# One 128-row transfer for each of the last output tiles instead of two of 64 rows, with a new order list for the compute jobs, in an attention and SwiGLU kernel

## The chip, the core and the metric

The kernel runs on one core of a Trainium2 chip. A core has a matrix engine (TensorE, in the profile PE, its weight loads PEld), a vector engine (VectorE, DVE), a scalar engine (ScalarE, ACT), a general engine (GpSimd, POOL) and a queue engine (SyncE, SP). Each runs its own list of instructions in order and waits for others through semaphores. Transfers to and from memory are issued here from the lists of SP, ACT and POOL, and all are carried by the same 16 DMA engines. Matrix products land in PSUM, which has eight banks of 128 rows by 512 floats; everything else on the chip lives in SBUF, 128 rows (partitions) wide.

The metric is device time in microseconds (us) of one execution, as the median of several runs. Lower is better.

## The reference

A linear attention with cosine weights feeds a SwiGLU block. Batch is 8, heads 8, sequence 576, head size 64; the block has 4608 tokens, width 512 and inner width 1536.

```
phi(x)  = concat(relu(x) * cos_w, relu(x) * sin_w)        # cos_w, sin_w by position
kv      = einsum('bhsf,bhsd->bhfd', phi(k), v)
z       = sum over s of phi(k)
num     = einsum('bhsf,bhfd->bhsd', phi(q), kv)
den     = einsum('bhsf,bhf->bhs',  phi(q), z) + 1e-6
x       = (num / den), heads side by side                 # [4608, 512]
g       = x @ w_gate
out     = (silu(g) * (x @ w_val)) @ w_out                 # [4608, 512], float32
```

## The kernel before

**Tiles and groups.** The 4608 tokens are cut into 72 pieces of 64 rows (`NH = B * NC`, `NC = 9` pieces for each batch). A tile `t` (0 to 35) is two pieces, 128 rows: piece `2t` on partitions 0 to 63, piece `2t + 1` on 64 to 127. Four tiles are a group `tg` (0 to 8). The output is seen as `out_v[b, c]`, one 64-row piece of 512 columns each, whose rows lie nine output rows apart.

**Stages.** For each tile the attention numerators and denominators are one PE job (`tile_jobs`, lines 784 and 789 in the profile), ACT and DVE divide (lines 803 to 820), and the result `x` is turned, either by a DMA transpose from SP (`turn_job`, line 749, `xT<-x`) or, for early tiles, by PE (line 757) with a copy by ACT (line 630). For each batch from the second on, `q` is made into features in `r_q`, with nine pieces by ACT (line 890), and turned by one DMA transpose from SP (line 852, `phit<-r_q`). For each group the gate and value products follow (lines 917, 990, 1065), then the output products (line 1275 for group 0, line 1155 for the others).

From group 1 on, products are made with seven block products in place of eight, of sums and differences of blocks. Within gate and value these are M1 to M7 (line 990), whose token-side sums X1 to X4 are made by DVE (`x_sum_jobs`, line 963, tile `kvt`, in the last group `raw_kv`). Within the output these are P1 to P7 (line 1155). M7 needs X3, and X3 needs the turned x of all four tiles of its group. An output block is ready as follows: columns 0 to 255 (`HD = 256`) of a group's first two tiles after P2 (job `e11`), columns 256 to 511 of its last two after P5 (`e22`), columns 0 to 255 of its last two after P4 (`e21`), and columns 256 to 511 of its first two after P3 (`e12`).

**The order of the work.** Work up to about 27 us is issued by a written sequence and stands ahead of the list that follows. All later work is cut into 1453 jobs with numbers in the order of their making. A job has an engine, a function that issues its instructions, and the jobs that it comes after. The string `ORDER` lists all job numbers; a letter picks an engine where there is a choice, and digits behind the colon pick a PSUM bank or another buffer. The jobs are issued in this order, so the list fixes the order on every engine and queue; the waits follow from the data. The numbers in `Job({...})`, `tail=` and `dma=` fed the planner that once wrote the list; as the list is written out, they change nothing in what is issued.

Jobs that the prediction speaks of, by number: 47 is an early output product of group 0 (tile 2, four of the inner chunks; line 1275). 99 turns tile 7's x on PE (line 757) and 100 copies it on ACT (line 630). 124 is the DMA transpose of batch 2's features (SP, line 852), 142 the attention product of tile 9 that reads it (line 789). 348 and 349 are X3 and X1 of group 2 (DVE, line 963), 354 is M7 of group 2 (line 990). 286 is P4 of group 1 (line 1155).

**The stores.** Group 0 stores by `store_jobs` from SP, groups 1 to 6 and the last two tiles of group 7 from POOL, the first two tiles of group 7 (28 and 29) from SP: two transfers a tile, one for each 64-row piece (line 1124). Group 8, the last, stores by blocks as they become ready, half of each from SP (partitions 0 to 63) and half from ACT (64 to 127): `store_two_jobs` (line 1253) moves 64 partitions of two tiles by 256 columns, 128 KB, and `store_tile_jobs` (line 1262) 64 partitions of one tile by 256 columns, 64 KB. So the end of SP's queue holds four issues of group 7 (line 1124) and six of group 8 (two of line 1253, four of line 1262), and the end of ACT's the other six of group 8. In the last group the blocks of `e22`, `e21` and `e12` are evicted by DVE, one tile at a time (lines 1212 and 636), `e11` by ACT (line 632).

Of the kernel before, what the change touches and what calls it, by code (L numbers as in the profile page):

```python
# [18 lines left out]
def kernel(  # L19
# [1098 lines left out]
    def store_jobs(t, after, put, queues, cols=slice(0, d_model)):  # L1118
        for e in range(2):
            q_ = queues[e]  # L1120

            def fn(j, e=e):
                idx = 2 * t + e
                {"POOL": nc.gpsimd, "SP": nc.sync, "ACT": nc.scalar}[j.eng].dma_start(  # L1124
                    out=out_v[idx // NC, idx % NC][:, cols], in_=ob_of(t)[e * SH:(e + 1) * SH, cols])
            Job({q_: 535 if q_ == "POOL" else 610}, fn, after=after, put=put, tail=1500.0, dma=(1450.0, 480.0))
# [6 lines left out]
    def pair_of(p):  # L1133
        return (ob_last if obs[p].kind == "last ob" else ob_all)[:, obs[p].at[0]]

    def out_jobs(tg, key):
# [68 lines left out]
        if last:  # L1205
            store_two_jobs(t0, slice(0, HD), [e11], ("SP", "ACT"))
# [7 lines left out]
        if last:  # L1214
            store_two_jobs(t0 + 2, slice(HD, d_model), e22, ("SP", "ACT"))
# [6 lines left out]
        if last:  # L1222
            for n in range(2):
                store_tile_jobs(t0 + 2, n, slice(0, HD), [e21[n]])
        else:
            for t in (t0 + 2, t0 + 3):
                store_jobs(t, e22 + e21, [rooms[1]], ("POOL", "POOL"))
# [8 lines left out]
        if last:  # L1236
            for n in range(2):
                store_tile_jobs(t0, n, slice(HD, d_model), [e12[n]])
        else:
            for t in (t0, t0 + 1):  # L1240
                store_jobs(t, [e11] + e12, [rooms[0]], ("SP", "SP") if tg == NTG - 2 else ("POOL", "POOL"))
# [5 lines left out]

    def store_two_jobs(t, cols, after, queues):
        for e in range(2):
            def fn(j, e=e):  # L1250
                (b, c), (b1, _) = divmod(2 * t + e, NC), divmod(2 * t + 2 + e, NC)
                assert b == b1
                {"SP": nc.sync, "ACT": nc.scalar}[j.eng].dma_start(
                    out=out_v[b, c:c + 3:2, :, cols].rearrange("c p f -> p c f"),
                    in_=pair_of(t // 2)[e * SH:(e + 1) * SH, :, cols])
            Job({queues[e]: 660}, fn, after=after, tail=1300.0, dma=(700.0, 560.0))

    def store_tile_jobs(t, i, cols, after, queues=("SP", "ACT")):
        for e in range(2):
            def fn(j, e=e):  # L1260
                b, c = divmod(2 * (t + i) + e, NC)
                {"SP": nc.sync, "ACT": nc.scalar}[j.eng].dma_start(
                    out=out_v[b, c][:, cols], in_=pair_of(t // 2)[e * SH:(e + 1) * SH, i, cols])
            Job({queues[e]: 620}, fn, after=after, tail=1300.0, dma=(700.0, 280.0))
# [36 lines left out]
    for lo, hi in ((0, 2), (2, 4)):  # L1301
        def fn(j, lo=lo, hi=hi):
            o = raws[1, "k"][:, lo:hi]
            relu_on(j.eng, o, o)
# [118 lines left out]
    for tg in range(1, NTG):  # L1423
# [43 lines left out]
        6:7 4:6 12:1 8:0 10:5 16:3 20:4 29 5:8 9:7 13:0 17:1 1:3 376 7 187 28 191 11 186 188 189 31 30 24:7 18:2 26:3  # L1467
        22:6 21:6 25:2 33 32 2:7 67:0 34:45 14:1 70a 36a 35a 38a 37a 3 27 380 19 68v 69 15 23 71 0 41:2 44 40:0 43
        72:340 84:7 78:561 39:1 42 73 74 75:3 85a 79 86 80 87v 81:2 88 76:3 77 45 101:7 89:560 95:341 47 90 96 377
        102a 378 91 92:3 97 48 82:5 93:6 55:1 83 94 98:0 192 193 109 190 103 110 113 381 114 46 99:1 51:3 52 49  # L1470
# [105 lines left out]
```

## Time and profile before

| | |
|---|---|
| time, median of 3 runs | 299.13 us (298.21 to 299.59) |
| the profiled execution's own time | 298.66 us |
| its span, first to last instruction | 296.8 us |
| granted TensorE clock, mean | 0.996 |
| transferred | 40.90 MB, 138 GB/s on average |
| stores from POOL (line 1124) | 52 of 128 KB, 532 ns of POOL each |
| stores from SP (line 1124) | 12 of 128 KB |
| DMA transposes of x from SP | 28, 4.1 us from issue to landing in the median |
| DMA transposes of the features from SP | 6, 10.3 us in the median |

How to read the views: in the busy time by stretch a row has its window in us, its length, then for each engine busy time and, in brackets, the count of instructions, then the granted clock, the DMA engines' share and GB/s. In the timeline a row has start, length, engine, line, operation, tiles written and read, and a count where neighbours are merged; in brackets the idle time before it and what ended that. `SPq` and `ACTq` are queue instructions, here issues of transfers. The chain of waits is read as start, length, and what the time went to. A row of DMA issues ends with the median time from issue to landing. In the rows of DMA queues, q1 is SP's queue and q10 ACT's, with packets, MB and the share of 16 engines. A matmul's length in a row holds its way through the array, so neighbours overlap.

### The profile page before, as it was taken

The page shows a single profiled execution, that of the slowest core. Times are in us where ns is not written, and L with a number is a line of the kernel's source. Part 1 is how long each engine was busy: PE and PEld are TensorE (multiplying, and loading weights), DVE is VectorE, ACT ScalarE, POOL GpSimd, SP SyncE. Part 2 cuts the span into 40 slices and gives each one's busy share as a digit, 9 for nine tenths or more (in the row PEclk, how much of TensorE's full clock was granted, in tenths as well). Part 3 has the DMA queues.
Part 4 walks back from the last instruction along what each step waited for, and adds up shares of the span by engine and source line. Part 5 has one row for each costly group of instructions (what it writes and reads, how often), then busy time and mean ns, then how long its engine had stood idle before and what let it go on. Part 6 is the DMA issues. An engine that isn't in the chain of part 4 may idle for free.

```text
span 296.8 us, 8157 instructions
## 1 busy us (share of the span) xinstructions
PE 290.1 (98%) x3292; PEld 237.7 (80%) x3292; DVE 252.9 (85%) x513; ACT 199.1 (67%) x423; POOL 69.1 (23%) x122
## 2 busy tenths in 40 slices
PE   8999999999999999999999999999999999999993
PEld 4697455665877888988898898888988898888882
DVE  7976889889987899999898977998778968968882
ACT  6664347978479868985499689976566555564630
POOL 7963530012015012213343020400050032002000
PEclk9999999999999999999999999999999999999998
DMA  7999999999969999599959947980270036000226
GB/s 255 232 196 198 202 206 209 229 202 155 170 149 171 199 209 144 102 172 148 209 118 159 197 68 131 208 146 2 38 171 8 2 89 127 0 2 18 55 53 161
DMA packets 71973, 40.90 MB, mean 138 GB/s; under 512 B 48768, under 2 KB 68736, under 8 KB 71936
## 3 DMA queue, kind: packets, MB, share of 16 engines
q0 software_dynamic: 24800, 24.39, 49.9%
q1 hardware_dynamic: 46528, 15.47, 27.6%
q10 hardware_dynamic: 608, 0.52, 0.6%
q8 instruction: 26, 0.43, 0.6%
q14 instruction: 11, 0.09, 0.1%
HBM read 37.75 MB, written 9.44 MB: 159 GB/s over the span
## 4 chain that ended last, share of the span: by engine, by line
PE 87%; DMA 9%; DVE 2%; issue 0%; DVEq 0%
PE banks L990 43%; PE banks L1155 23%; DMA xT<-x 4%; DMA phit<-r_q 4%; PE banks L440 4%; PE banks L917 4%; PE banks L1275 3%; PE banks L789 3%; PE banks L718 2%; PE banks L1065 2%; DMA wo_sb<-in_v_dram 1%; DVE v L292 1%; PE banks L371 1%; PE banks L784 1%; PE banks L1323 0%; PE banks L314 0%
## 5 line engine op out<-in xcount | busy, mean ns | idle before, releaser
L1124 POOL DMA_DIRECT2D out_dram<-ob x52 | 27.3, 532 | 128.4 <-ACT ob L632 87.6
L630 ACT COPY banks<-banks 128x512 f32<-128x512 f32 (+1 forms) x53 | 30.4, 577 | 22.3 <-PE banks L990 9.9
L1049 ACT ACTIVATE sg<-banks 128x512 bf16<-128x512 f32 x72 | 40.9, 599 | 5.8 <-PE banks L990 5.6
L1085 DVE TENSOR_TENSOR ht<-sg,banks 128x512 f16<-128x512 bf16 x60 | 40.4, 682 | 4.8 <-PE banks L990 4.4
L1155 PEld LDWEIGHTS <-ht 128*128 128x128 f16 x384 | 37.5, 98 | 4.5
L990 PEld LDWEIGHTS <-wg_sb 128*128 128x128 f16 x384 | 36.7, 98 | 5.3
L990 PEld LDWEIGHTS <-wgs_sb 128*128 128x128 f16 x368 | 35.4, 98 | 6.4 <-issue 0.5
L1010 DVE TENSOR_TENSOR banks<-m,banks 128x512 f32<-128x512 f32 x44 | 30.2, 692 | 7.3 <-PE banks L990 6.0
L990 PEld LDWEIGHTS <-wv_sb 128*128 128x128 f16 x320 | 31.2, 98 | 3.7
L990 PE MATMUL banks<-kvt,wgs_sb 128*128 128x256 f16 x236 | 33.8, 273 | 0.3 <-DVE kvt L963 0.3
L1155 PEld LDWEIGHTS <-sums 128*128 128x128 f16 x288 | 28.0, 98 | 3.4
L630 ACT COPY m<-banks 128x512 f32<-128x512 f32 x44 | 25.5, 590 | 5.7 <-PE banks L990 5.7
L990 PE MATMUL banks<-xT,wg_sb 128*128 128x256 f16 x192 | 28.6, 273 | 0.0
L632 ACT ACTIVATE ob<-banks 128x512 f32<-128x512 f32 x32 | 19.1, 596 | 10.6 <-PE banks L1155 9.3
L1155 PE MATMUL banks<-wo_sb,ht 128*128 128x256 f16 x192 | 25.2, 273 | 0.0
L990 PE MATMUL banks<-kvt,wg_sb 128*128 128x256 f16 x168 | 24.4, 273 | 0.0
L1155 PE MATMUL banks<-wt_sb,sums 128*128 128x256 f16 x192 | 24.2, 273 | 0.0
L820 DVE TENSOR_TENSOR x<-banks,rec 128x512 f16<-128x512 f32 x31 | 21.3, 690 | 3.1 <-PE banks L990 0.5
L990 PE MATMUL banks<-xT,wv_sb 128*128 128x256 f16 x160 | 23.8, 273 | 0.0
L1155 PE MATMUL banks<-wt_sb,ht 128*128 128x256 f16 x192 | 22.8, 272 | 0.0
L890 ACT ACTIVATE r_q<-raw_q,tanq 128x256 bf16<-128x256 bf16 x45 | 20.1, 507 | 0.0
L292 DVE TENSOR_TENSOR v<-raw_kv,tab 128x1152 bf16<-128x1152 bf16 x27 | 19.9, 750 | 0.0
(160 smaller groups left out, 540.1 us busy)
## 6 DMA issues: line engine op xcount, KB each, us to landing
out_dram<-ob POOLq DMA_DIRECT2D x52, 128.0 KB, 3.3
raw_kv<-in_k_dram POOLq DMA_DIRECT2D x7, 576.0 KB, 6.2
raw_q<-in_q_dram POOLq DMA_DIRECT2D x12, 288.0 KB, 9.9
raw_kv<-in_v_dram POOLq DMA_DIRECT2D x6, 576.0 KB, 9.3
out_dram<-ob SPq DMA_DIRECT2D x12, 128.0 KB, 2.8
wg_sb<-in_moe_w_gate_dram POOLq DMA_DIRECT2D x5, 256.0 KB, 9.0
wv_sb<-in_moe_w_val_dram POOLq DMA_DIRECT2D x5, 256.0 KB, 9.6
wo_sb<-in_v_dram SPq DMA_DIRECT2D x2, 576.0 KB, 4.1
```

Source lines behind the costliest of these rows:

```text
L292: nc.vector.tensor_tensor(out=v2s[b == 1][:, g, :, :, 0:D], in0=(first if b == 0 and g == 0 else {"v": raw_of(b, "v")})["v"][:, g].unsquee ...
L440: nc.tensor.matmul(out=st["f", tg, fc, lo][i], lhsT=(wg_sb, wv_sb)[i][:, kc, fs], rhs=xT[tg][:, ts, kc], start=(kc == 0), stop=(kc == KC - 1))
L630: nc.scalar.copy(out=out, in_=in_)
L632: nc.scalar.mul(out=out, in_=in_, mul=mul)
L820: tt(out=x_.rearrange("p (i y d) -> p i y d" if pairs else "p (y e d) -> p e y d", d=D, **({"i": 2} if pairs else {"e": 2})), in0=view()[: ...
L890: nc.scalar.activation(out=home()[:, :, c, 1], in_=raws[b, "q"][:, :, c], func=AF.Relu, scale=tanq[:, c:c + 1])
L990: nc.tensor.matmul(out=to[:, i], lhsT=a[:, c, 2 * u + i], rhs=x()[:, :, c], start=first and i == 0 and c == 0, stop=c == KH - 1, skip_grou ...
L1010: tt(out=bank(c), in0=one(m7_all, m).rearrange("p i x -> p (i x)"), in1=bank(b), op=ALU.add)
L1049: nc.scalar.activation(out=gates(rooms[w])[:, :, jh * HT:(jh + 1) * HT], in_=src, func=AF.Silu, scale=DOWN)
L1085: tt(out=ht[:, 4 * u + w:4 * u + w + 3:2, jh * HT:(jh + 1) * HT], in0=gates(rooms[w])[:, :, jh * HT:(jh + 1) * HT], in1=src.rearrange("p ( ...
L1124: {"POOL": nc.gpsimd, "SP": nc.sync, "ACT": nc.scalar}[j.eng].dma_start(out=out_v[idx // NC, idx % NC][:, cols], in_=ob_of(t)[e * SH:(e + ...
L1155: nc.tensor.matmul(out=to, lhsT=a[:, kc, i * P:(i + 1) * P], rhs=b[:, kc], start=first and kc == 0 and i == 0, stop=kc == HC - 1, skip_gro ...
```

## The change

**Stores.** A new function `whole_tile_job` stores 128 partitions of one tile, both 64-row pieces, by one transfer. Tiles 28 and 29 use it from SP for all 512 columns (256 KB each). The last group uses it for each tile and half of the columns (128 KB each), the first tile of a pair from SP and the second from ACT. `store_two_jobs` and `store_tile_jobs` go. Where the right half of tile 34 waited for both evictions of `e22`, each tile now waits for its own. Stores from POOL stay as they are. There are 1447 jobs in place of 1453.

**Order.** `ORDER` is a new list. Job numbers up to 1308 mean the same job in both lists; later ones are shifted by the jobs that went. On PE 379 of 490 jobs stand at another place in the engine's order (by up to 14 places), on ACT and DVE most of some 390 and 440 (by up to 24 and 28). The relu jobs 68 and 87 change between ACT and DVE. POOL's order is the same. On SP the DMA transposes keep their order; among the stores at the end, tile 29's comes first, then tile 28's, then those of the last group, where before the second half of tile 28 came first, then its first half, the second half of tile 29, the first store of group 8, and the first half of tile 29. The order of the last group's products on PE was P5 of both tiles, then P4 of both; now the first half of P4 stands ahead of P5. SP's stores of the last group are, in order, tile 32 left (columns 0 to 255), 34 right, 34 left, 32 right; ACT's are 35 right, 33 left, 35 left, 33 right.

```diff
     def store_jobs(t, after, put, queues, cols=slice(0, d_model)):
+        if len(queues) == 1 and 2 * t % NC < NC - 1:
+            return whole_tile_job(t, cols, after, queues[0], put, 6500.0)
         for e in range(2):
-            q_ = queues[e]
+            q_ = queues[e % len(queues)]
...
-            Job({q_: 535 if q_ == "POOL" else 610}, fn, after=after, put=put, tail=1500.0, dma=(1450.0, 480.0))
+            Job({q_: 560}, fn, after=after, put=put, tail=6500.0, dma=(1270.0, 480.0))
+
+    def whole_tile_job(t, cols, after, queue, put=(), tail=1300.0):
+
+        def fn(j):
+            b, c = divmod(2 * t, NC)
+            {"POOL": nc.gpsimd, "SP": nc.sync, "ACT": nc.scalar}[j.eng].dma_start(
+                out=out_v[b, c:c + 2][:, :, cols], in_=ob_of(t)[:, cols])
+        Job({queue: 600}, fn, after=after, put=list(put), tail=tail, dma=(700.0, 560.0))
...
         if last:
-            store_two_jobs(t0, slice(0, HD), [e11], ("SP", "ACT"))
+            for n in range(2):
+                whole_tile_job(t0 + n, slice(0, HD), [e11], ("SP", "ACT")[n])
...
         if last:
-            store_two_jobs(t0 + 2, slice(HD, d_model), e22, ("SP", "ACT"))
+            for n in range(2):
+                whole_tile_job(t0 + 2 + n, slice(HD, d_model), e22[n:n + 1], ("SP", "ACT")[n])
...
         if last:
             for n in range(2):
-                store_tile_jobs(t0 + 2, n, slice(0, HD), [e21[n]])
+                whole_tile_job(t0 + 2 + n, slice(0, HD), [e21[n]], ("SP", "ACT")[n])
...
         if last:
             for n in range(2):
-                store_tile_jobs(t0, n, slice(HD, d_model), [e12[n]])
+                whole_tile_job(t0 + n, slice(HD, d_model), [e12[n]], ("SP", "ACT")[n])
         else:
             for t in (t0, t0 + 1):
-                store_jobs(t, [e11] + e12, [rooms[0]], ("SP", "SP") if tg == NTG - 2 else ("POOL", "POOL"))
+                store_jobs(t, [e11] + e12, [rooms[0]], ("SP",) if tg == NTG - 2 else ("POOL", "POOL"))
...
-    def store_two_jobs(t, cols, after, queues):
...
-    def store_tile_jobs(t, i, cols, after, queues=("SP", "ACT")):
...
     ORDER = """
-        6:7 4:6 12:1 8:0 10:5 16:3 20:4 29 5:8 9:7 13:0 17:1 1:3 376 7 187 28 191 11 186 188 189 31 30 24:7 18:2 26:3
...
+        8:2 4:4 12:1 10:0 14:3 24:7 20:6 16:5 5:2 9:0 13:1 29 21:5 25:3 17:4 0 376 28 377 378 11 191 15 6:1 26:0 22:7
...
-        1424:1 1425:2 1430 1431 1432 1433 1434 1437 1438 1435 1436 1439 1445 1442 1440 1446 1444 1447 1441 1443 1449
-        1450 1448 1451 1452
...
+        1427 1422:7 1423:2 1435 1429 1430 1437 1431 1432 1433 1436 1441 1438 1439 1434 1428 1440 1442 1443 1444 1445
+        1446
     """
```

More of the change, by code (lines that the diff above doesn't have):

```diff
@@ L1246, in out_jobs @@
         J_["ht_free", tg, 1, 1] = P4 + ts[1]
-    def store_two_jobs(t, cols, after, queues):
[L1249 to L1256, printed above, removed]
-    def store_tile_jobs(t, i, cols, after, queues=("SP", "ACT")):
[L1259 to L1264, printed above, removed]
     def plain_out_jobs(key):
@@ L1466 @@
     ORDER = """
-        6:7 4:6 12:1 8:0 10:5 16:3 20:4 29 5:8 9:7 13:0 17:1 1:3 376 7 187 28 191 11 186 188 189 31 30 24:7 18:2 26:3
-        22:6 21:6 25:2 33 32 2:7 67:0 34:45 14:1 70a 36a 35a 38a 37a 3 27 380 19 68v 69 15 23 71 0 41:2 44 40:0 43
-        72:340 84:7 78:561 39:1 42 73 74 75:3 85a 79 86 80 87v 81:2 88 76:3 77 45 101:7 89:560 95:341 47 90 96 377
-        102a 378 91 92:3 97 48 82:5 93:6 55:1 83 94 98:0 192 193 109 190 103 110 113 381 114 46 99:1 51:3 52 49
[63 rows of a table removed]
+        8:2 4:4 12:1 10:0 14:3 24:7 20:6 16:5 5:2 9:0 13:1 29 21:5 25:3 17:4 0 376 28 377 378 11 191 15 6:1 26:0 22:7
+        67:4 68a 70a 31 30 33 32 186 7 1:6 27 69 23 380 187 34:23 41:4 44 18:0 71 19 35a 37a 36a 38a 72:670 78:121
+        84:0 40:5 73 79 87a 85a 74 80 75:0 81:1 86 39:3 43 76:6 2:7 89:010 101:2 42 90 102a 3 88 91 92:3 188 45 93:2
[64 rows of a table added]
     """
```

123 rows, old and new, of the table ORDER are left out of this document.

## The prediction

> **What bounds the kernel now.** I read the page, then the busy time by stretch, the waits of PE (two in the body, shown in brackets in part two), the chain of waits, and the timeline around each gap and at the end.
>
> ```profile
> span 296.8 us, 8157 instructions
> PE 290.1 (98%) x3292; PEld 237.7 (80%) x3292; DVE 252.9 (85%) x513; ACT 199.1 (67%) x423; POOL 69.1 (23%) x122
> ...
> 26.90:291.90 265.00, 264.30 (x2963) 219.04 (x2960) 230.47 (x446) 183.17 (x388) 50.36 (x90) 1.00 0.74 129
> ...
> 152.25 12.23 PE banks L990 x112
> ...
> 282.68 9.18 PE banks L1155 x84
> 291.89 0.42 DVE r_q L636
> ```
>
> The listed jobs run from 26.9 us to the last matmul at 291.9. In these 265.0 us PE is idle for 0.7, at full clock (1.00); 112 matmuls take 12.23 us, 0.109 each, with nothing between. So the body is PE's own work, which the change leaves as it is: moving jobs can win back only PE's few waits. The second stage with a price is the end: the last eviction ends at 291.89 + 0.42 = 292.31, the span at 296.8, and in these 4.5 us only stores run. The profiled execution took 298.66, 1.86 more than its span; it lies 0.47 under the median of 299.13.
>
> **The change, part one: the stores.** The end of before:
>
> ```profile
> 287.96 0.60 ACT L632 ACTIVATE r_q<-banks 128x512 f32<-128x512 f32 x1 [2.02 <-PE banks L1155]
> 288.62 0.42 DVE L1212 SCALAR_TENSOR_TENSOR r_q<-banks,r_q 128x256 f32<-128x256 f32 x1 [0.66 <-PE banks L1155]
> ...
> 291.24 0.42 DVE L636 TENSOR_SCALAR r_q<-banks 128x256 f32<-128x256 f32 x1 [0.23 <-PE banks L1155]
> 291.89 0.42 DVE L636 TENSOR_SCALAR r_q<-banks 128x256 f32<-128x256 f32 x1 [0.23 <-PE banks L1155]
> ...
> 288.58 0.65 SPq L1253 DMA_DIRECT2D out_dram<-r_q  x1
> 289.28 0.61 SPq L1124 DMA_DIRECT2D out_dram<-ob  x1
> 289.99 1.16 SPq L1253 DMA_DIRECT2D out_dram<-r_q  x1
> 291.24 3.17 SPq L1262 DMA_DIRECT2D out_dram<-r_q  x4
> ...
> 288.59 2.56 ACTq L1253 DMA_DIRECT2D out_dram<-r_q  x2
> 291.25 2.82 ACTq L1262 DMA_DIRECT2D out_dram<-r_q  x4
> ...
> L1262 SPq DMA_DIRECT2D out_dram<-r_q x4: 467/546/550, 291.2 to 293.9; - x4
> ...
> out_dram<-ob SPq DMA_DIRECT2D x4, 128.0 KB, 2.4
> out_dram<-r_q ACTq DMA_DIRECT2D x2, 128.0 KB, 3.9
> out_dram<-r_q SPq DMA_DIRECT2D x4, 64.0 KB, 2.0
> ```
>
> SP's last four issues take from 291.24 to 294.41. The last has only the eviction of 292.31 to wait for, but goes out at 293.9 and lands 2.0 later, at 295.9: 3.6 us after its data. So the stores are backed up, by issues and by data. By data:
>
> ```profile
> 289.75:290.50 0.75, 0.75 (x10) 0.67 (x8) 0.42 (x1) 0.00 (x0) 0.00 (x0) 1.00 0.69 142
> 290.50:291.50 1.00, 1.00 (x12) 0.89 (x10) 0.69 (x2) 0.00 (x0) 0.00 (x0) 1.00 0.84 274
> 291.50:292.50 1.00, 0.35 (x4) 0.07 (x1) 0.58 (x2) 0.00 (x0) 0.00 (x0) 1.00 0.64 138
> 292.50:293.50 1.00, 0.00 (x0) 0.00 (x0) 0.00 (x0) 0.00 (x0) 0.00 (x0) 1.00 0.88 285
> 293.50:294.75 1.25, 0.00 (x0) 0.00 (x0) 0.00 (x0) 0.00 (x0) 0.00 (x0) 0.98 0.79 194
> ...
> ## 3 DMA queue, kind: packets, MB, share of 16 engines
> q1 hardware_dynamic: 124, 0.13, 66.5%
> q10 hardware_dynamic: 10, 0.01, 3.2%
> ...
> q10 hardware_dynamic: 236, 0.21, 64.3%
> q1 hardware_dynamic: 103, 0.07, 23.8%
> ```
>
> The first queue pair is the stretch 291.6 to 292.5, the second 292.5 to 293.5. The rate (last column, GB/s) steps between 138 and 285. When SP's queue (q1) moves alone, that is rows 0 to 63 of a tile, it is near 140; when ACT's queue (q10), rows 64 to 127, moves as well, it is near 280. A transfer of 128 rows holds both halves by itself, so I take 280 for it, and keep 140 as the other end.
>
> The Trainium skill, "SBUF — State Buffer", section Door 1, says that DMA bandwidth depends on how many of 16 SBUF ports the rows reach, and that rows 0 to 63 reach eight of them, 0 to 127 all. By that rule the new stores run at the fast rate from first to last, and the backlog below is gone before the last store; without it the slow rows would have to stand, 194 or worse. The trace agrees with it as far as the two kinds of stretch show.
>
> Removed: of SP's 10 issues behind group 7 and 8 remain 6, of ACT's 6 remain 4. Moved, though the list is said to move no transfer: the store of tile 29, whose second half went out at 289.28 between the last group's stores, now stands with tile 28's ahead of them, in the quiet time from 285. So 128 KB less compete after 288.58. Also, product P4's first half now runs ahead of P5's, so the columns of tile 34 that come from P4 are evicted first.
>
> Now the queue. Evictions end about every 0.65 us from 289.04 (288.62 + 0.42) to 292.31. SP issues tile 32's left half at 288.58 (the eviction of 287.96 has ended), then tile 34's right half at 289.7, then its left half and at 291.66 tile 32's right half: free in time. ACT starts with tile 35's right half, whose eviction now ends at 290.35 (289.04 + 2 x 0.65), and behind this waiting instruction stands tile 33's left half, ready since 288.56 and thus 2.4 us later than it could be; then tile 35's left half, then tile 33's right half, the last. An issue costs between 0.55 (the 546 ns of L1262's row) and 1.28 (2.56 / 2); I take the 0.65 of the first L1253, of as many rows by columns. Three from 290.35 end at 292.3, so the last goes out at 292.35.
>
> Data: the first store's bytes move by 290.5, seven transfers of 131 KB (0.92 MB) follow. From issue to first bytes it takes about 1.2 us (288.58 to the busy stretch from 289.75), so they flow from about 290.9; at 280 GB/s all issued work is through by 294.2, so the last store is not held. It lands 2.0 to 3.9 after its issue; I take the 2.4 of a lone 128 KB store, as nothing is left beside it: 294.75, against 295.9. The tail gains **1.1 us**. Ends: a landing of 2.0 gives 1.55; the backlog at 194 GB/s ends at 290.9 + 4.7 = 295.6, landing some 0.35 later, so nothing is gained (-0.05); at 140 it ends at 297.4, a loss of 1.9.
>
> **Part two: the moved jobs.** Most PE, ACT and DVE jobs stand at another place, by up to 14, 24 and 28 places. POOL's order is the same, SP's but for tile 29. Each move is free as long as its operands come before PE does; the price of one that fails is a wait of the size of the two that exist:
>
> ```profile
> 63.87 0.60 PE L990 MATMUL banks<-kvt,wg_sb 128*128 128x256 f16 x4
> ...
> 64.78 0.69 PE L789 MATMUL banks<-kv,phit 128*128 128x65 bf16 x16 [0.32 <-DMA phit<-r_q]
> ...
> 81.65 0.60 PE L1155 MATMUL banks<-wt_sb,sums 128*128 128x256 f16 x4
> 82.10 0.76 DVE L963 TENSOR_TENSOR kvt<-xT 128x512 f16<-128x512 f16 x2 [0.98 <-DMA xT<-x]
> 82.58 1.47 PE L990 MATMUL banks<-kvt,wgs_sb 128*128 128x256 f16 x12 [0.34 <-DVE kvt L963]
> ...
> 47.84 1.63 ACT L630 COPY xT<-banks 128x512 f16<-128x512 f16 x3
> 49.36 1.70 ACT L890 ACTIVATE r_q<-raw_q,tanq 128x256 bf16<-128x256 bf16 x4
> ...
> 48.46 0.39 PE L757 MATMUL banks<-ident,x 128*128 128x128 f16 x4
> ...
> 53.56 11.17 DMA phit<-r_q
> ...
> 69.92 12.09 DMA xT<-x
> ```
>
> (The first of these rows is from a stretch that ends at 65.1: four matmuls from 63.87, 0.44 us.) Start to start the gaps are 64.78 - 64.31 = 0.47 and 82.58 - 82.09 = 0.49: **0.96** is all that the body can give.
>
> The second gap: product M7 of group 2 (job 354) needs X3, which DVE starts at 82.10 once tile 10's turned x has landed (69.92 + 12.09 = 82.01). The new list puts exactly one more PE job ahead of 354: P4 of group 1 (job 286), 12 matmuls, 1.31 us. PE then comes at 82.09 + 1.31 = 83.40, or 82.93 if the first gap is gone too. On DVE X1 now goes before X3, which so ends with that pair, at 82.10 + 0.76 = 82.86. The cover is just enough even if nothing lands earlier: -0.49.
>
> The first gap: the same PE work stands ahead of tile 9 (job 142), so only an earlier landing helps. SP sends the transpose at 53.56 behind ACT's nine pieces, which run without a break from the eviction of tile 7's turned x; that waits for PE at 48.46. The new list takes job 47 (four matmuls of 512 columns, 0.86 us) from ahead of it. If ACT follows and the landing time of 11.17 stays, the transpose lands up to 0.86 earlier, and 0.47 suffices. Whether a transfer in a full DMA stretch lands earlier for being sent earlier, no row shows: between 0 and -0.47, I take -0.2, under half.
>
> The rest: any other of the moved jobs may come late; the trace shows only that the old places wait nowhere else. Bounds: 0, and +0.5, one gap more. I take 0. Part two: **-0.7**, from -0.96 to +0.5.
>
> **Sum.** 298.66 - 1.1 - 0.7 = 296.9. As the profiled execution lies 0.47 below the median, the median of after should be at 296.9 to 297.4: **297.1**.
>
> **Rivals.**
>
> A: the data rate rules the tail. The 128-row stores move no faster than the alternating halves did (194): tail 0, 298.66 - 0.7 + 0.2 of offset = **298.2**. For it: the slow stretches make up half of the tail. Against: whenever both halves moved, the rate doubled.
>
> B: the moved jobs bring as many waits as they take away: 298.66 - 1.1 + 0.2 = **297.8**. For it: most places are new. Against: one more gap has to open for each that closes, and DVE and ACT have 0.15 and 0.33 of the span free.
>
> C, slower: ACT's queue is the bound. Three issues stand behind the wait for tile 35, at the 1.28 of the L1253 pair each: 290.35 + 3.8 = 294.2 for the last issue, landing 3.9 later (the 128 KB row of ACT) at 298.1, a loss of 2.2: 298.66 + 2.2 - 0.7 = **300.2**. It decides from an issue cost of (295.9 - 2.4 - 290.35) / 3 = 1.05 on. For it: issues of 1.16 and an average of 1.28 are there; against: the first L1253 on SP took 0.65, and the long ones came while the DMA engines were full.
>
> **Chances.** Forecast 0.60 (own range 296.3 to 297.9), A 0.17, B 0.15, C 0.08. Range 296.1 to 298.9: tail and body both at their better end at the bottom (298.66 - 1.55 - 0.96), at the top neither part gains (298.66 + 0.24 of offset); C lies outside. Half a per cent, 1.5 us, is what a measurement here can tell: faster means below 297.6. That is nearly nine tenths of the forecast, half of B, little of A: 0.62; slower, above 300.6, is a part of C: 0.03.
>
> **What would show it.** Right: SP's and ACT's last issue within 0.2 us of the last eviction, the last landing about 2.4 later, and over 250 GB/s from 291 to 294; no wait of PE at L789 on phit nor at L990 on kvt. Wrong: ACT's last issue a microsecond after the last eviction (C), rates under 200 while 128-row stores move (A), new lines in PE's list of waits (B).

## The result and the profile after

| | before | after |
|---|---|---|
| time, median of 4 runs each on the same chip | 299.04 us | **321.78 us** (321.27 to 322.94) |
| ratio | | 1.0769 (95% interval 1.0729 to 1.0808) |
| the profiled execution's own time | 298.66 | 322.08 |
| span | 296.8 | 320.2 |
| first listed PE job starts | 26.89 | 27.21 |
| from there to the end of PE's last product | 264.96 | 265.73 |
| last eviction ends | 292.31 | 293.40 |
| from there to the end of the span | 4.5 | **26.8** |

The change is slower by 22.7 us, far outside the range of 296.1 to 298.9. Of the 23.4 us between the two spans, 0.3 lie ahead of the list, 0.8 in the listed work and 22.3 behind the last eviction, where only stores run. The page of after shows it in the last four of the 40 slices (8.0 us each):

```profile
span 320.2 us, 8152 instructions
...
PE   8999999999999999999999999999999999995000
...
PEclk9999999999999999999999999999999999999555
DMA  7999999989989967999795979026006200201111
GB/s 269 213 199 197 203 207 218 228 149 174 165 140 204 220 98 140 185 129 177 150 163 110 150 169 177 2 32 167 3 2 139 61 2 0 68 11 53 48 48 38
```

From 26.9 to 200 us the DMA engines are full (a share of 1.02) and move 170 GB/s on average. In the tail they are one tenth busy, though nothing else is left to do, and move 48. (The clock of 0.5 stands behind the end of PE's work.) The busy time by stretch of the tail, with the DMA share and GB/s in the last two columns:

```profile
289.00:293.00 4.00, 3.94 (x37) 3.28 (x34) 2.18 (x7) 0.60 (x1) 0.00 (x0) 1.00 0.15 55
293.00:300.00 7.00, 0.00 (x0) 0.00 (x0) 0.40 (x1) 0.00 (x0) 0.00 (x0) 0.68 0.13 50
300.00:310.00 10.00, 0.00 (x0) 0.00 (x0) 0.00 (x0) 0.00 (x0) 0.00 (x0) 0.50 0.14 48
310.00:318.00 8.00, 0.00 (x0) 0.00 (x0) 0.00 (x0) 0.00 (x0) 0.00 (x0) 0.50 0.14 48
```

A share of 0.13 is 2 of 16 engines (0.125). It is the same whether SP's queue (q1) moves alone, as from 292 to 294.5 (the first two lines), or ACT's (q10) moves as much, as from 300 to 316:

```profile
DMA packets 62, 0.13 MB, mean 51 GB/s; under 512 B 0, under 2 KB 0, under 8 KB 62
q1 hardware_dynamic: 62, 0.13, 13.0%
...
DMA packets 766, 0.77 MB, mean 48 GB/s; under 512 B 12, under 2 KB 766, under 8 KB 766
q1 hardware_dynamic: 384, 0.39, 6.8%
q10 hardware_dynamic: 382, 0.39, 6.8%
```

The ten stores hold 2 x 262,144 + 8 x 131,072 bytes, 1.57 MB; at 48 GB/s that is 32.8 us, and from the first issue at 284.05 that reaches to 317, most of the way to the span's end at 320.2. The timeline of SP and ACT and DVE's last eviction:

```profile
284.05 1.19 SPq L1134 DMA_DIRECT2D out_dram<-ob  x2
289.67 15.66 SPq L1134 DMA_DIRECT2D out_dram<-r_q  x4
...
291.51 12.71 ACTq L1134 DMA_DIRECT2D out_dram<-r_q  x4
...
292.98 0.42 DVE L636 TENSOR_SCALAR r_q<-banks 128x256 f32<-128x256 f32 x1 [0.23 <-PE banks L1165]
```

Four issues now take 15.66 and 12.71 us. The first one or two on each queue go out in 0.5 to 1.1 us; the later ones are held for 3.7 to 5.5 us each, while the transfers ahead of them are not through. The DMA part of the page, for the stretch from 284 to 322, gives what may be a second count of the engines:

```profile
DMA packets 1302, 1.60 MB, mean 42 GB/s; under 512 B 20, under 2 KB 1044, under 8 KB 1300
...
q1 hardware_dynamic: 780, 1.05, 7.8%
q10 hardware_dynamic: 520, 0.52, 3.9%
```

The data packets hold 1 or 2 KB (a row of 256 or 512 floats). Beside them stand 20 packets under 512 bytes, two for each of ten transfers.

So the theory to test, called E below: a transfer is divided among the engines by its outermost step in memory. The old stores walk 64 rows; the new one, `out_v[b, c:c + 2][:, :, cols]`, walks two pieces first and 64 rows inside, so its outermost step has 2 values and it runs on 2 engines. Its rivals: the new list makes the tail (L), or a transfer of 128 rows is slow in itself (W).

### The profile page after: what moved, and what is told of

Same layout as the page of the kernel before. It is cut to its first block, busy times and chain, and to the rows that moved or that the text cites. A ratio compares the mean times of both kernels' runs of the same rounds, so it can differ in the third digit from the quotient of the medians.

```text
span 320.2 us, 8152 instructions
## 1 busy us (share of the span) xinstructions
PE 291.1 (91%) x3292; PEld 238.1 (74%) x3292; DVE 252.3 (79%) x511; ACT 200.9 (63%) x425; POOL 70.2 (22%) x122
## 4 chain that ended last, share of the span: by engine, by line
PE 85%; DMA 4%; ACT 1%; DVE 1%; issue 0%; ACTq 0%
PE banks L990 40%; PE banks L1165 23%; PE banks L1065 4%; PE banks L440 3%; PE banks L1269 3%; DMA wo_sb<-in_moe_w_out_dram 3%; PE banks L186 3%; PE banks L789 2%; PE banks L718 2%; DMA xT<-x 2%; PE banks L917 1%; PE banks L371 1%; PE banks L314 0%; ACT sg L925 0%; ACT m L630 0%
## 5 line engine op out<-in xcount | busy, mean ns | idle before, releaser
L1049 ACT ACTIVATE sg<-banks 128x512 bf16<-128x512 f32 x72 | 42.3, 595 | 12.3 <-PE banks L990 11.9
L1165 PE MATMUL banks<-wt_sb,sums 128*128 128x256 f16 x192 | 25.2, 273 | 0.0
```

The lines of the kernel that those rows point to most:

```text
L1049: nc.scalar.activation(out=gates(rooms[w])[:, :, jh * HT:(jh + 1) * HT], in_=src, func=AF.Silu, scale=DOWN)
L1165: nc.tensor.matmul(out=to, lhsT=a[:, kc, i * P:(i + 1) * P], rhs=b[:, kc], start=first and kc == 0 and i == 0, stop=kc == HC - 1, skip_gro ...
```

## The experiments

**Two transfers of 64 rows in the new list** (`halves`).

```diff
-                out=out_v[b, c:c + 2][:, :, cols], in_=ob_of(t)[:, cols])
+            for e in range(2):
...
+                    out=out_v[b, c + e][:, cols], in_=ob_of(t)[e * SH:(e + 1) * SH, cols])
```

> The changed kernel with its list, but each of the ten whole-tile stores sent as two transfers of 64 rows on the same queue, one behind the other. Theory E (few engines): the store of 128 rows writes to memory in a pattern whose outermost step has only 2 values (the two 64-row pieces), and is carried by 2 of the 16 DMA engines; with 64 rows the outermost step has 64 values and all engines carry it. Then the body ends as in the changed kernel (293.4) and the tail is about that of before (4.5), with two to four more issues a queue perhaps 1 more: 293.4 + 4.5 to 5.5 + 1.86 = 299.8 to 300.8, and the last stretch moves at 140 to 280 GB/s. Rival L (the list): the new order of the stores and jobs makes the tail; then nothing changes, 321 to 322. Rival W (width): any single transfer of 128 rows is slow in itself; then also 299.8 to 300.8, and this run does not tell E from W.

Measured: 301.30 us, ratio to before 1.0085 (1.0066 to 1.0105). The tail falls from 26.8 to 6.4 us. L is out.

```profile
293.00:297.00 4.00, 0.30 (x3) 0.02 (x1) 0.54 (x2) 0.00 (x0) 0.00 (x0) 0.88 0.70 167
```

```profile
DMA packets 1602, 1.60 MB, mean 42 GB/s; under 512 B 320, under 2 KB 1344, under 8 KB 1600
```

First the stretch behind 293, then the packets: a share of 0.70, and 320 small packets for 20 transfers, 16 each. It came out 0.5 above what was expected. That fits the issues: each queue now has eight behind 290 (SP's take 6.29 us, ACT's end at 297.6).

**Whole tiles in the old list** (`whole_old`).

```diff
+    def store_whole(j, t, cols):
+        b, c = divmod(2 * t, NC)
+        {"SP": nc.sync, "ACT": nc.scalar}[j.eng].dma_start(out=out_v[b, c:c + 2][:, :, cols], in_=ob_of(t)[:, cols])
...
-                    out=out_v[b, c:c + 3:2, :, cols].rearrange("c p f -> p c f"),
-                    in_=pair_of(t // 2)[e * SH:(e + 1) * SH, :, cols])
+                store_whole(j, t + e, cols)
```

> The kernel before with its own list, but with the ten stores of whole tiles in place of the halves, at the places of the old stores (tiles 28 and 29 of group 7 from SP, the eight blocks of group 8 by SP for the first tile of a pair and by ACT for the second). Theory E and rival W: the list is innocent; the body ends at 292.3 as before, and the tail of 22 us more comes back: 319 to 321, with 48 GB/s at the end. Rival L: the tail stays about that of before, 297 to 300.

Measured: 323.60 us, ratio 1.0828 (1.0809 to 1.0848). The tail is back without the new list, at the rate of after:

```profile
300.00:310.00 10.00, 0.00 (x0) 0.00 (x0) 0.00 (x0) 0.00 (x0) 0.00 (x0) 0.50 0.14 49
```

That is 2.6 above what was expected. Its span is 1.8 longer than that of after, and 1.6 of this is the first store, which leaves at 285.68, in after at 284.05.

**128 rows, pattern turned around** (`perm64`).

```diff
-                out=out_v[b, c:c + 2][:, :, cols], in_=ob_of(t)[:, cols])
+                out=out_v[b, c:c + 2][:, :, cols].rearrange("c (s q) f -> s c q f", s=64), in_=ob_of(t)[:, cols])
```

> The changed kernel, with one transfer of 128 rows a tile as there, but the memory pattern turned around: outermost 64 steps, then the two pieces. So the 128 rows of each of these ten stores are written to the same 128 output rows in another sequence, and the output rows of those tiles are exchanged among themselves. Theory E: outermost 64 means all 16 engines, over 140 GB/s at the end, and the tail ends as early as the prediction had it or as before: 293.4 + 2.5 to 4.5 + 1.86 = 297.8 to 299.8. Rival W: a transfer of 128 rows is as slow as in the changed kernel: 320 to 322. Rival L: also 320 to 322.

Measured: 298.61 us, ratio 0.9997 (0.9984 to 1.0010): 23 us less than after, with as many transfers, bytes and partitions, the same queues and the same list. W is out. The stretches, ACT's issues and the packets:

```profile
291.00:293.00 2.00, 2.00 (x21) 1.75 (x18) 1.31 (x4) 0.00 (x0) 0.00 (x0) 1.00 0.39 130
293.00:296.00 3.00, 0.23 (x3) 0.00 (x0) 0.47 (x2) 0.00 (x0) 0.00 (x0) 1.00 0.80 263
```

```profile
291.81 2.74 ACTq L1134 DMA_DIRECT2D out_dram<-r_q  x4
```

```profile
DMA packets 1442, 1.60 MB, mean 42 GB/s; under 512 B 160, under 2 KB 1184, under 8 KB 1440
```

160 small packets for ten transfers, 16 each; four issues of ACT take 2.74 us in place of 12.71; 263 GB/s on average with the last stores under way. The tail is 3.7 us, 0.8 less than before. Since rows are exchanged within the tiles, this run and those like it show where the time goes; they are no kernels to use.

**How the time goes with the outermost step** (`rows64_2`, `rows64_4`, `rows64_8`): two transfers of 64 rows a tile as in the first run, with the rows written in 2, 4 or 8 sweeps. The edit against `halves`, for 2:

```diff
-                    out=out_v[b, c + e][:, cols], in_=ob_of(t)[e * SH:(e + 1) * SH, cols])
+                    out=out_v[b, c + e][:, cols].rearrange("(q k) f -> k q f", k=2), in_=ob_of(t)[e * SH:(e + 1) * SH, cols])
```

> As the run with two transfers of 64 rows for each tile, but each writes its 64 rows in two sweeps, first every other one and then the rest, so that the outermost step has 2 values again; the 64 output rows of each piece are exchanged among themselves. Theory E: 2 engines again, 1.57 MB at 48 GB/s from about 285.3, 33 us: last landing near 318 to 320, time 320 to 323. Rival W: transfers of 64 rows are fast, 299.8 to 300.8.

> As the run that wrote each 64 rows in two sweeps, but in four sweeps, each with every fourth row: the outermost step has 4 values; the 64 output rows of each piece are exchanged among themselves. Theory E: 4 engines, twice the 48 GB/s, 96 to 100. Tiles 28 and 29 (0.52 MB from 285.3) are through at 290.5, the 1.05 MB of group 8 then follow without a break until 301: time about 303 to 305. Rival S (rows written out of sequence are slow, whatever the count): 322 as with two sweeps.

> The same in eight sweeps, every eighth row: the outermost step has 8 values. Theory E: 8 engines, about 195 GB/s: group 7's part is through at 288, group 8's 1.05 MB take 5.4 us and are held by their issues as in the run with two plain transfers of 64 rows: 300.5 to 302. Rival S: 322.

| outermost step | time | ratio to before | small packets a transfer | DMA share and GB/s, stretch from 293 |
|---|---|---|---|---|
| 2 | 322.83 | 1.0810 (1.0792 to 1.0828) | 40 / 20 = 2 | 0.13, 50 |
| 4 | 307.21 | 1.0270 (1.0250 to 1.0289) | 80 / 20 = 4 | 0.27, 94 |
| 8 | 302.13 | 1.0107 (1.0090 to 1.0124) | 160 / 20 = 8 | 0.49, 149 |
| 64 (`halves`) | 301.30 | 1.0085 (1.0066 to 1.0105) | 320 / 20 = 16 | 0.70, 167 |

The rows behind it, with 2 values:

```profile
293.00:300.00 7.00, 0.00 (x0) 0.00 (x0) 0.00 (x0) 0.00 (x0) 0.00 (x0) 0.81 0.13 50
```

```profile
DMA packets 1322, 1.60 MB, mean 42 GB/s; under 512 B 40, under 2 KB 1064, under 8 KB 1320
```

with 4:

```profile
293.00:303.00 10.00, 0.22 (x3) 0.00 (x0) 0.45 (x2) 0.00 (x0) 0.00 (x0) 0.70 0.27 94
```

```profile
DMA packets 1362, 1.60 MB, mean 42 GB/s; under 512 B 80, under 2 KB 1104, under 8 KB 1360
```

and with 8:

```profile
293.00:297.00 4.00, 0.00 (x0) 0.00 (x0) 0.35 (x1) 0.00 (x0) 0.00 (x0) 0.94 0.49 149
```

```profile
DMA packets 1442, 1.60 MB, mean 42 GB/s; under 512 B 160, under 2 KB 1184, under 8 KB 1440
```

E holds: share and packets follow the count, and 64 rows with 2 sweeps are as slow as 128 rows were. S is out, since four and eight sweeps are out of sequence too. An engine moves 25 GB/s with 2, 24 with 4 and 19 with 8 (50 / 2, 94 / 4, 149 / 8). Sizes were missed: with 4 the time is 2 above what was expected, as the stores of tiles 28 and 29 moved at 46 GB/s up to 288 and all stores at 85 up to 291, not at 96 from the start; why was not tried. With 8 the eight engines are full (0.49 is 8 of 16) and ACT's issues end only at 297.5, so this run does not tell whether the engines or the issues hold its end.

**The list alone** (`perm64_old`): `whole_old` with the pattern turned around in `store_whole`, so that rows are written in the same sequence as in `perm64`.

> The list of before with ten stores of whole tiles, each with the memory pattern turned around (outermost 64 steps); the 128 output rows of each of these tiles are exchanged among themselves. It differs from the run with the same stores in the changed kernel (298.61, ratio to before 0.9997) by the list alone. Theory M (the new list costs about as much as the stores gain): the tail is about 3.7 as there, the body ends 0.6 earlier: about 298.0, ratio 0.996 to 0.998. Rival P (the list gains 0.7, as the prediction had it): 299.3, ratio 1.002. A ratio of 0.999 to 1.001 says that the lists differ by less than the runs show.

Measured: 298.17 us, ratio 0.9972 (0.9959 to 0.9984). M holds. By the quotient of the two ratios, 0.9997 / 0.9972, the new list costs 0.25% (0.07 to 0.43% when the two intervals are added as squares), some 0.75 us. The list is nearly all that differs: the right half of tile 34 here still waits for both evictions of `e22`, in `perm64` for its own.

**Stores of 64 rows in the old list, arranged otherwise** (`fewer_old`, `t29_old`, `two_all`). `t29_old` only swaps two jobs in `ORDER`: the half of tile 29 that stood behind the first store of group 8 goes ahead of it. (The expectations and the prediction call it the second half. It is the second to be sent, and holds the tile's first 64 rows.) `fewer_old` also stores the columns after `e21` by two transfers as after `e22`; `two_all` does that for the columns after `e12` too.

```diff
-        1418:6 1406 1411 1412 1413 1409 1420 1426 1422 1423 1427 1308 1421:1 1428:0 1310 1309 1312 1429 1311 1410 1414
+        1418:6 1406 1411 1412 1413 1409 1420 1426 1422 1423 1427 1308 1421:1 1428:0 1310 1309 1312 1311 1429 1410 1414
```

> The list of before with its stores of 64 rows, but the columns 0 to 255 of the last pair of tiles (after e21) go by two transfers of 64 rows of both tiles in place of four of one, and the second half of tile 29 is issued ahead of the first store of group 8. Two issues fewer on the queues behind 290, all 16 engines. Theory I (the tail of before is held by the queues' issues): the last issue comes 0.6 to 1 earlier, at about 292.4 to 293.3, the last landing 0.5 to 1.2 earlier, 297.8 to 298.5, ratio 0.996 to 0.998. Rival D (the data set the end): the same bytes, the same end: 298.7, ratio 1.000.

> The kernel before with one job moved: the second half of tile 29 is issued from SP ahead of the first store of group 8, in the quiet time after 287, in place of behind it. This is the one store that the change moved although it was said to move none. If the bytes that compete behind 288.6 or SP's one issue less there hold the end (part of theory I), 0.3 to 0.6 less than before: 298.4 to 298.7, ratio 0.998 to 0.999. If the last evictions and their own stores alone set the end: ratio 1.000.

> The run with fewer issues in the list of before (298.32, ratio 0.9979), and in addition the last blocks (after e12) by two transfers of 64 rows of both tiles, one from SP and one from ACT, in place of four of one tile. Theory I: the last issue then comes with the last eviction, 0.5 earlier than there, and the time is 297.8 to 298.2, ratio 0.996 to 0.9975. Rival D: now all of the last 256 KB wait for the last eviction, 131 KB more than there behind it, 0.47 at 280 GB/s, which takes the gain back: ratio 0.9975 to 0.999.

| | time | ratio to before | behind the last eviction |
|---|---|---|---|
| `t29_old` | 298.57 | 0.9980 (0.9970 to 0.9991) | 3.9 |
| `fewer_old` | 298.32 | 0.9979 (0.9964 to 0.9993) | 3.7 |
| `two_all` | 298.89 | 1.0005 (0.9991 to 1.0019) | 4.1 |

Sending this half of tile 29 ahead gives 0.6 us (0.3 to 0.9); two issues fewer on top of it give nothing that can be told. Fewer still gives the gain back, though the last issues of `two_all` end no later than those of `fewer_old`:

```profile
291.38 1.94 ACTq L1264 DMA_DIRECT2D out_dram<-r_q  x2
...
291.38 1.90 SPq L1264 DMA_DIRECT2D out_dram<-r_q  x2
```

```profile
292.25 1.28 SPq L1269 DMA_DIRECT2D out_dram<-r_q  x2
```

Here (first `two_all`, then `fewer_old`) SP ends at 293.28 and 293.53, after evictions that end at 292.66 and 292.84. So the number of issues is not what holds the end of `fewer_old`; the bytes that can only leave behind the last eviction (rival D) fit. The loss is 0.26% between the two ratios, some 0.8 us, and D's 0.47 lies within their intervals. That D is the cause is argued from this, not tried by itself. `t29_old` and `fewer_old`, which write every row in its place, are the two kernels that are faster than before (by 0.2%) and than after. No run stores whole tiles, every row in its place, on all engines.

**Four jobs of the new list** (`four_jobs`). In all six profiles of the new list two products near 136 or 137 us start some 0.16 late each, with no engine named. In `perm64` (timeline of PE, then two rows of DVE):

```profile
136.40 0.60 PE L990 MATMUL banks<-xT,vsums 128*128 128x256 f16 x4
137.00 0.60 PE L990 MATMUL banks<-kvt,wv_sb 128*128 128x256 f16 x4
137.59 0.60 PE L990 MATMUL banks<-xT,wgs_sb 128*128 128x256 f16 x4
138.03 0.60 PE L990 MATMUL banks<-kvt,wv_sb 128*128 128x256 f16 x4
138.46 1.04 PE L1165 MATMUL banks<-wo_sb,ht 128*128 128x256 f16 x8
...
136.26 0.69 DVE L1010 TENSOR_TENSOR banks<-m,banks 128x512 f32<-128x512 f32 x1
136.86 0.68 DVE L1018 TENSOR_TENSOR m<-m,banks 128x512 f32<-128x512 f32 x1
```

```diff
...
-        597:6 518 610:1 517 611 613 586 584 599 601 523:45 618 590 585:8 612:7 600 589 524 604:45 605 525 527 587 616
-        602 614 630:1 591 622 620 623 615:6 624 619 514 490 495 500 710:3 631 633:6 469 470 468 476 474 656 477 475
+        597:6 518 610:1 517 611 613 586 584 599 601 523:45 618 590 585:8 612:7 600 589 524 604:45 605 525 527 602 587
+        614 616 630:1 591 622 620 623 615:6 624 619 514 490 495 500 710:3 631 633:6 469 470 468 476 474 656 477 475
...
```

> The run with the changed kernel's list and whole-tile stores turned around to 64 outermost steps (rows exchanged within each of these tiles), and in the list four neighbouring PE jobs of group 3 in another order: the products with weight blocks vsums, wv, wgs, wv become wgs, vsums, wv, wv, as in the list of before. In that run 0.32 us stood before two of them (0.60 in place of 0.44 from start to start, at 137.0 and 137.6), which the trace puts to no other engine. Theory F (a fixed cost of this order on PE): both gaps go, wv and wv run on without a break, 0.3 us less between the first of the four and the next product. Rival T (something at that time or behind those places in the program): 0.15 to 0.32 stays, at the same or neighbouring jobs. The time itself, 298.3 against 298.6, is below what one run tells.

Measured, one run: 299.33 us beside 299.72 of before, from which nothing can be told. The same stretch:

```profile
136.86 0.60 PE L990 MATMUL banks<-xT,wgs_sb 128*128 128x256 f16 x4 [1.14 <-DVE m L1018]
137.30 0.60 PE L990 MATMUL banks<-xT,vsums 128*128 128x256 f16 x4
137.73 1.04 PE L990 MATMUL banks<-kvt,wv_sb 128*128 128x256 f16 x8
138.61 1.04 PE L1165 MATMUL banks<-wo_sb,ht 128*128 128x256 f16 x8
...
136.13 0.68 DVE L1018 TENSOR_TENSOR m<-m,banks 128x512 f32<-128x512 f32 x1
```

From the first of the four to the next product it is 1.75 in place of 2.06: both gaps go with the order. That does not make them a fixed cost, as F had it, for the DVE rows point to a wait. In `perm64` DVE's two sums end at 136.95 and 137.54, and each late product starts 0.05 behind one of them; in the other five profiles of the new list it is the same, to 0.01. In `four_jobs` the product that now comes first starts 0.05 behind the second sum (136.13 + 0.68 = 136.81), and here the profile names this sum as what it waited for, 1.14 us. So the small gaps are very likely waits for DVE too, which the view leaves unnamed because the matmuls ahead of them still count as busy. The order of the new list spreads the wait over two products; undone alone, it costs more in this execution, whose listed PE work takes 266.2 us.

## Why the prediction was wrong, step by step

**The failed step** is "A transfer of 128 rows holds both halves by itself, so I take 280 for it, and keep 140 as the other end." Both rates came from transfers whose outermost step has 64 values. The new store has another memory pattern, outermost 2, and moved at 48 to 50: a third of the lower end. The bound was taken from the nearest rows without asking whether the new transfer would have the same engines as those. The rows themselves were misread too. In the fast stretch ACT's queue carries 0.21 of the 0.28 MB, so rows 64 to 127 alone moved at about 210 GB/s, and the stretch does not show 128 rows as twice 64. All that hung on the step fell: the forecast, the range and the chance of slower. The range was also narrower than the working: it stops at 298.9, while the working's own worse ends, 1.9 in the tail and 0.5 in the body, lead to 298.66 + 1.9 + 0.5 = 301.1. The working size was in reach: before's stretch of 285 GB/s at a share of 0.88 is 285 / (0.88 x 16) = 20.2 GB/s an engine. Two engines then need 1.57 / 0.0404 = 39 us for the ten stores, and from SP's first issue at 285.2 that ends near 324, where after ended at 320.2.

The Trainium skill, "DMA: Bandwidth & Descriptors", section "Why a DMA increments its semaphore by 16 and not by 1", says it: the number of engines is the largest up to 16 that divides the sizes of the slowest dimension, other than 1, of both patterns. The runs here agree, with 2, 4, 8 and 16 small packets a transfer for outermost sizes of 2, 4, 8 and 64. The Trainium skill's rule on ports that the prediction drew on ("SBUF — State Buffer", section Door 1) speaks of the rows on the chip's side. The new stores do span both halves, but at 2 engines that did not matter: 128 rows (after) and 64 rows (`rows64_2`) both moved at 50 GB/s from 293 to 300.

**The rest of part one was near the mark once all engines carry the store.** In `perm64` ACT's four issues take 0.69 each on average (0.65 was taken), the rate behind 293 is 263 (280), and the tail is shorter by 0.8 (`perm64_old` 1.1; the prediction 1.1). The half of tile 29 that moved gives 0.2% by itself (`t29_old`). That transfers of 128 rows cost the engines less time than those of 64, once all engines carry them, is also shown, by the stores of tiles 28 and 29, alone on SP's queue from 285.5 to 288.2 (first `halves`, then `perm64`):

```profile
q1 hardware_dynamic: 319, 0.52, 84.7%
q1 hardware_dynamic: 288, 0.52, 51.8%
```

The same bytes keep the engines busy for 0.85 of the stretch in transfers of 64 rows and for 0.52 in transfers of 128. Still, `perm64` at 298.61 is 1.5 above the forecast of 297.1. That fits the smaller gain in the tail and what part two lost.

**Part two had the wrong sign.** The two waits priced at 0.96 us are not in after's list of waits of PE behind 27 us, which has one other:

```profile
PE banks L990 <- DMA xT<-x: 0.6, 1, 0.6
```

It stands at 139.1, for tile 17's turned x. Over all profiles, from PE's first listed job to the end of its last product:

| list | executions | us, each | mean |
|---|---|---|---|
| old | before, `whole_old`, `perm64_old`, `fewer_old`, `t29_old`, `two_all` | 264.96, 264.69, 264.75, 264.39, 265.16, 265.11 | 264.84 |
| new | after, `halves`, `perm64`, `rows64_2`, `rows64_4`, `rows64_8` | 265.73, 265.83, 264.89, 265.30, 265.33, 265.16 | 265.37 |

The new list is longer by 0.53 (0.19 is the standard error of that difference), not shorter by 0.7. Of the two waits, the second went as forecast: PE's wait for X3 (line 990 on `kvt`) is listed in four of the six profiles of the old list and in none of the six of the new. The first comes and goes with the execution, not only with the list: tile 9's wait for phit is listed in three of the old six, not in `fewer_old` for one, and stands again in `rows64_2`, which has the new list:

```profile
PE banks L789 <- DMA phit<-r_q: 0.3, 1, 0.3
```

So one of the two was priced from a single profile as if it belonged to the list. And the term put at 0, the other moved jobs, was not 0: the new list has late starts of its own, such as the one at 139.1 and the 0.32 near 137. The waits that the profile lists behind 27 us are even fewer with it (2.0 us over its six profiles, 2.8 over the six of the old list), so its loss is in time that the list of waits does not show. It was not traced job by job, and its cause stays open but for the gaps near 137.

**The rivals.** A had the right place (the data rate rules the tail) with a price of 298.2, since its 194 came from the same old transfers. B is right for the body, and a little worse than even. C, the only slower one, is out: ACT's issues were long in after because the transfers ahead of them were, and take 2.74 us for four in `perm64`.

## What to carry to other kernels

Before a transfer's rate is taken from the profile, read the shape of both its patterns: in these stores from SP and ACT the size of the outermost step decided how many engines carried them, and fewer, wider transfers were slower because they put a small step outside. Stores from POOL were not tried. In a profile the sign of k engines is a DMA share of k/16 that stays flat while transfers are pending, and k small packets a transfer. A wait seen in one execution is worth pricing only if it is there in several.

## What was not expected of the hardware

- Transfers from both queues, SP's and ACT's, together stayed at a share of 0.13 to 0.15 in after, each at half the rate that SP's had alone: with 2 engines each they did not spread to 4, so it seems that both used the same two.
- An issue on SP or ACT took up to 5.5 us in after and 7.5 in `whole_old`, while transfers were pending on two engines. With four engines (`rows64_4`, stores of half the size) the last group's took 0.5 to 1.3, with all of them (`perm64`) 0.5 to 0.8.
- The start ahead of the list, the same code in all runs, ended between 26.86 and 28.34 us, a scatter of 1.5 us, larger than all that the list could give. The listed PE work itself scatters by 0.8 and 0.9 us within each list, so no single pair of profiles shows an effect of half a us there.
